# Second layer of the block in seven products: four of seven units summed over two neighbouring quads in a PSUM bank

## The chip, the cores and the metric

One core of a Trainium2 chip. The metric is device microseconds of one execution. Engines: PE is TensorE (PEld its weight loads), DVE VectorE, ACT ScalarE, POOL GpSimd, and SP issues nearly all DMAs.

## The reference, cut

```python
x = performer_attention(q, k, v, omega)          # [2304, 512]
P = sinkhorn(exp(x @ w_gate))                    # [2304, 8], 8 rounds
out = zeros(2304, 512)
for e in range(8):                               # w1: 8 x 512 x 1024, w2: 8 x 1024 x 512
    h = maximum(x @ w1[e], 0)
    out += P[:, e:e+1] * (h @ w2[e])
h = out @ w_in                                   # w_in 512 x 2048, float64 in DRAM
return (h - tanh(h)) @ w_out                     # w_out 2048 x 512, float64 in DRAM
```

All in float32 accuracy: each factor is held as a high part (float32r) and a low part, and a product is three matmuls, high by high, high by low, low by high.

## The kernel before, in words

Attention runs first (to about 170 us). Then come stages: the sum over the eight experts for three blocks of 768 tokens, s = 0, 1, 2, and the last two layers for the same three blocks.

**The expert stages.** The 8 x 1024 hidden columns are cut into 32 quads of 256 columns. For a quad the first layer (512 x 256 weights against 512 x 768 tokens, seen as 2 x 2 blocks) is made with seven block products in place of eight, in Winograd's form. Each product is six matmuls of 128 x 128 by 384 columns (`product`, L1089); three PSUM banks a, b and e take them. In s = 0 the second layer is plain (L1356). In s = 1 and s = 2 it too is made with seven products: `quad7` makes seven forms of h, H[0] to H[6], each high and low half (`high` on ACT, `low` on POOL, L1173), and each unit i multiplies H[i] with a summed piece of w2 and adds to the accumulator `xacc[i]` (SBUF, two halves d of 128 x 384). At the end of a block `join` adds the seven accumulators to the four blocks of the result and stores them.

**Order around the change.** The program order of each engine is the order in which the code is run (manual schedule). A quad has seven steps: a first-layer product, then `between(k)`, which runs unit UORD[k] of the previous quad (`Second.run(k)`), UORD = 5, 0, 4, 3, 2, 1, 6, and then two ticks. A unit is two groups of three matmuls, one for each half d, each in a bank of its own. For d = 1 ACT copies the accumulator into the bank beforehand (`load`, L1248), the matmuls add to it, and ACT copies it back (L1269). For d = 0 DVE adds the bank to the accumulator (L1275); in s = 2 three of the seven are "light": ACT copies the bank out (L1279) and POOL adds it (L1280). After a unit `post(k)` makes the next forms of h: the subtractions that give t1 (L1216) and t3 (L1220) on DVE, one on POOL (L1222), t4 (L1227), and their splits. PSUM's eight banks are five for the first layer (tag q) and three for the second (tag l). h has nine buffers.

**Weights.** A generator, `weights()`, is advanced once by each tick. For quad a it loads the first layer's seven pieces u (split once in s = 0 and kept in DRAM, `st1`) and the second layer's seven pieces y of quad a - 1 (`st2`). Two y pieces share a tile; there are six tiles, and a tile is granted when both units of the tile six before are used. During s = 1 four of the seven y pieces (units 1, 2, 3, 5) are new: POOL makes four sums of raw w2 (`sums_of`, L202 to L205), ACT and POOL (for unit 2 DVE) split each (L89, L92), and the piece is stored for s = 2 when two later ones wait. `convert` turns w_in and w_out from float64 bits to float32 on DVE (L1054 to L1066), ACT and POOL in the later part of s = 0 and in s = 2, one step on 24 of 32 and 18 of 32 ticks. The last stage's loads of them wait until all is converted.

## Time and profile before

| | us |
|---|---|
| median of 3 runs | 2267.24 (2261.35 to 2270.09) |
| the profiled execution | 2264.46 |
| its span, first to last instruction | 2262.4 |
| PE busy in the span | 2071.4 |
| DVE, ACT, POOL busy | 1731.7, 1376.3, 1607.7 |

PE's busy time counts every stretch in which a matmul is under way; matmuls overlap, so it is no measure of how fast they follow each other. The times of steps are read from the starts of matmuls in the timeline.

### The profile page before, as it was taken

What the parts mean: (1) busy time and instruction counts of PE and PEld (TensorE: products, weight loads), DVE (VectorE), ACT (ScalarE), POOL (GpSimd) and SP (SyncE); (2) the same over time, 40 slices, a digit from 0 to 9 for tenths busy, and PEclk for the clock granted to TensorE, in tenths of its full rate; (3) what the DMA queues carried; (4) which work ended last, traced back from release to release, by engine and by line L of the source; (5) the groups of instructions that cost most, each with busy time, mean ns of one, the idle gap of its engine ahead of it and who ended that gap; (6) DMA issues with size and microseconds to landing.
All of it is one profiled execution on the core that took longest, in us unless ns stands there. A gap on an engine that the chain in (4) does not pass through costs nothing.

```text
span 2262.4 us, 37383 instructions
## 1 busy us (share of the span) xinstructions
PE 2071.4 (92%) x11408; PEld 1902.6 (84%) x11408; DVE 1731.7 (77%) x3277; ACT 1376.3 (61%) x3337; POOL 1607.7 (71%) x1961
## 2 busy tenths in 40 slices
PE   9999999999997988888888688888888879999999
PEld 7777988999987888888888688888888868998998
DVE  8884868888864666666666587888778769999997
ACT  7883333444433666666666366666666667888885
POOL 7866878878744777777767677777777797565552
PEclk9999999999998999999999799999999999999999
DMA  6538787788756778777787577877778723132210
GB/s 167 145 116 281 272 281 265 265 285 284 260 188 212 239 245 289 239 256 252 243 261 234 183 249 251 276 253 245 238 249 251 226 98 110 53 116 75 90 52 33
DMA packets 341368, 470.85 MB, mean 208 GB/s; under 512 B 70944, under 2 KB 164784, under 8 KB 341168
## 3 DMA queue, kind: packets, MB, share of 16 engines
q1 hardware_dynamic: 335568, 461.85, 62.4%
q10 hardware_dynamic: 5600, 6.61, 0.8%
q8 instruction: 91, 1.49, 0.3%
q14 instruction: 109, 0.89, 0.1%
HBM read 328.29 MB, written 140.06 MB: 207 GB/s over the span
## 4 chain that ended last, share of the span: by engine, by line
PE 49%; DVE 15%; POOL 13%; ACT 7%; DMA 7%; issue 6%; SPq 2%; DVEq 0%; POOLq 0%; ACTq 0%
PE l L1356 16%; PE b L1089 8%; PE Y L1261 6%; PE e L1089 5%; PE X L1261 5%; PE p L1318 4%; PE a L1089 3%; DMA st<-y 3%; POOL h L1173 3%; ACT h L1170 2%; POOL tmp L513 1%; POOL h L1222 1%; SPq L252 1%; POOL s L203 1%; DVE t L1339 1%
## 5 line engine op out<-in xcount | busy, mean ns | idle before, releaser
L1356 PE MATMUL l<-v,h 128*128 128x512 f32 x2016 | 485.1, 394 | 8.0 <-ACT h L1344 2.7
L1356 PEld LDWEIGHTS l<-v,h 128*128 128x128 f32 x2016 | 377.0, 189 | 86.6 <-ACT h L1344 4.3
L1261 PE MATMUL Y<-h,y 128*128 128x384 f32 x1290 | 313.9, 347 | 113.6 <-ACT Y L1248 66.9
L1269 ACT COPY seven<-Y 128x384 f32<-128x384 f32 x430 | 206.8, 481 | 301.0 <-PE Y L1261 297.3
L1089 PE MATMUL b<-x,u 128*128 128x384 f32 x1728 | 357.5, 342 | 10.1 <-DVE t L1183 9.7
L1261 PE MATMUL X<-h,y 128*128 128x384 f32 x1398 | 327.9, 345 | 35.7 <-DVE seven L1275 24.1
L1261 PEld LDWEIGHTS Y<-h,y 128*128 128x128 f32 x1290 | 226.9, 190 | 145.5 <-ACT Y L1248 87.4
L1089 PEld LDWEIGHTS b<-x,u 128*128 128x128 f32 x1728 | 314.3, 193 | 15.7 <-DVE t L1183 10.0
L1173 POOL TENSOR_TENSOR h<-t,h 128x384 fp32r<-128x384 f32 x224 | 232.4, 1038 | 104.0 <-ACT h L1170 55.9
L1275 DVE TENSOR_TENSOR seven<-X,seven 128x384 f32<-128x384 f32 x345 | 190.2, 552 | 151.2 <-PE X L1261 149.4
L1261 PEld LDWEIGHTS X<-h,y 128*128 128x128 f32 x1398 | 254.8, 193 | 45.9 <-DVE seven L1275 31.4
L1173 POOL TENSOR_TENSOR h<-h,h 128x384 fp32r<-128x384 f32 x192 | 204.0, 1063 | 47.9 <-ACT h L1170 46.6
L1089 PE MATMUL a<-x,u 128*128 128x384 f32 x1152 | 233.5, 337 | 1.5 <-ACT u L89 1.5
L1089 PE MATMUL e<-x,u 128*128 128x384 f32 x1152 | 232.7, 336 | 0.0
L1318 PE MATMUL p<-x,u 128*128 128x384 f32 x1152 | 211.7, 339 | 0.0
L1248 ACT COPY Y<-seven 128x384 f32<-128x384 f32 x430 | 209.3, 487 | 0.4
L1318 PEld LDWEIGHTS p<-x,u 128*128 128x128 f32 x1152 | 205.2, 190 | 3.4
L1089 PEld LDWEIGHTS a<-x,u 128*128 128x128 f32 x1152 | 204.0, 189 | 2.8 <-ACT u L89 2.2
L1089 PEld LDWEIGHTS e<-x,u 128*128 128x128 f32 x1152 | 204.4, 189 | 0.0
L92 POOL TENSOR_TENSOR v<-rs,v 128x256 fp32r<-128x256 f32 x176 | 144.3, 848 | 64.4 <-ACT v L89 57.8
L1345 POOL TENSOR_TENSOR h<-t,h 128x384 fp32r<-128x384 f32 x94 | 97.5, 1037 | 121.7 <-ACT h L1344 116.5
L1170 ACT CAST h<-t 128x384 fp32r<-128x384 f32 x224 | 115.5, 516 | 50.2 <-POOL t L1227 24.3
(245 smaller groups left out, 4060.5 us busy)
## 6 DMA issues: line engine op xcount, KB each, us to landing
u<-st SPq DMA_DIRECT2D x448, 256.0 KB, 4.5
y<-st SPq DMA_DIRECT2D x320, 256.0 KB, 4.1
st<-u SPq DMA_DIRECT2D x224, 256.0 KB, 4.3
rs<-in_moe_w_dram SPq DMA_DIRECT2D x128, 256.0 KB, 3.6
st<-y SPq DMA_DIRECT2D x128, 256.0 KB, 4.8
st<-v SPq DMA_DIRECT2D x96, 256.0 KB, 5.3
rq<-in_moe_w_dram SPq DMA_DIRECT2D x32, 512.0 KB, 4.9
rqi<-win SPq DMA_DIRECT2D x24, 512.0 KB, 4.6
```

The source lines that it names most:

```text
L92: eng.tensor_tensor(dst[:, 1, i : i + w], src[:, i : i + w], dst[:, 0, i : i + w].bitcast(F32), ALU.subtract)
L203: G.tensor_tensor(s2, s1, a11, ALU.subtract)
L1089: nc.tensor.matmul(ps[:, :TB], u[:, wi, c], x[:, xi, c], start=(start and m == 0), stop=(stop and m == 5), skip_group_check=True,)
L1170: nc.scalar.copy(H[k][:, 0], src)
L1173: eng.tensor_tensor(H[k][:, 1], src, H[k][:, 0].bitcast(F32), ALU.subtract)
L1248: nc.scalar.copy(ps, xacc[UORD[k]][:, 1])
L1261: nc.tensor.matmul(ps, u[:, wi, d * P : (d + 1) * P], h[:, hi], start=(j == 0 and not pre), stop=(j == 2), skip_group_check=True,)
L1269: nc.scalar.copy(X[:, d], ps)
L1275: nc.vector.tensor_tensor(X[:, d], ps, X[:, d], ALU.add)
L1318: nc.tensor.matmul(ps, u1[f + i][:, wi, c], ux[state["x0"] + 2 * t + i][:, xi, c], start=(m == 0), stop=(m == 11))
L1345: nc.gpsimd.tensor_tensor(lo, s, hi.bitcast(F32), ALU.subtract)
L1356: nc.tensor.matmul(ps, hh[f][:, hi, t : t + P], u2[n + f][:, wi], start=(f == 0 and i == 0), stop=(f == len(hh) - 1 and i == 2),)
```

## The change

The second layer is planned by slots (7 for a quad) in place of `Second`. Units 0 and 6 of an even quad and of the odd one before it, and units 5 and 4 of an odd quad and of the even one before it, are summed in one bank: a group of six matmuls for each half d, in two different slots. Both halves of these are preloaded and copied back by ACT. Units 1, 2 and 3 stay two groups of three a quad; their d = 0 is added by DVE, their d = 1 goes through ACT for unit 2 (s = 1) or all three (s = 2), and through DVE otherwise. Light adds are gone. A quad's units run in slots 1 to 8 after its end (1, 2: the first pair unit; 3, 4, 5, 6; 7 is the next quad's slot 0) in place of 0 to 6. The third subtraction (t3) moves into `post(0)`. The joins come one or two slots later. In s = 1 and s = 2 there are four and four banks; before and after, five and three. h has five buffers for halves that are used up in the next quad and four for those held for two. Unit 5's new piece of an even quad is split into a spare place and only stored, and is read back for the next, odd quad; the other pieces are asked for in the order in which they are used. Stores are issued three ticks after the piece. Conversion in s = 0 stops one quad later; in s = 2 its steps are finer (8 a piece in place of 6) and taken on 22 of 32 ticks. The nine slots after the last quad run within the first four pieces of the last stage.

```diff
+    stores = []
+    def store(dst, src):
+        stores.append([2, dst, src.bitcast(F32)])
+    def send(age):
+        for x in stores:
+            x[0] -= 1
+        while stores and stores[0][0] < age:
+            nc.sync.dma_start(*stores.pop(0)[1:])
+    def second_units(R):
+        r = R % NQ
+        if r == 0:
+            return [(0, R), (3, R), (2, R), (1, R), (6, R)]
+        if r % 2 == 0:
+            return [(0, R - 1), (0, R), (3, R), (2, R), (1, R), (6, R - 1), (6, R)]
+        units = [(5, R - 1), (5, R), (4, R - 1), (4, R), (3, R), (2, R), (1, R)]
+        return units[:4] + [(0, R)] + units[4:] + [(6, R)] if r == NQ - 1 else units
...
                 if a == 1:
-                    flush()
+                    send(9)
...
-                for i in range(7):
-                    if a < NG:
+                R = a - 1
+                units = second_units(R) if a else []
+                if fresh and R % 2 == 0:
+                    units.append((5, -1))
+                for i in range(max(7, len(units))):
+                    if a < NG and i < 7:
...
-                    if not a:
...
-                    m = 7 * (a - 1) + i
+                    o, g = units[i]
...
+                    u = two[:, m % 2]
+                    if g < 0:
+                        spentw.add(m)
                     else:
-                        two = uw[m - 1][1]
-                    u, o = two[:, m % 2], UORD[i]
-                    uw[m] = u, two
-                    st = st2[(a - 1) % NQ][:, o]
-                    if fresh and o in src:
+                        uw[o, g] = u, m
+                    m += 1
+                    if fresh and (g < 0 or g == R and o in (1, 2, 3, 5)):
                         split(u, src[o], nc.vector if o == 2 else G)
-                        store(st, u)
+                        store(st2[R][:, o], u)
                         yield None
                     else:
-                        nc.sync.dma_start(u.bitcast(F32), st)
+                        nc.sync.dma_start(u.bitcast(F32), st2[g % NQ][:, o])
...
+    def set_banks(name, nq, nl):
+        banks.close()
+        ppm[:] = [banks.enter_context(tc.tile_pool(name=name, bufs=nq, space=PSUM, reuse_waits="tile")), nl]
+    set_banks("ppm", 5, 3)
...
+    hp_ = ctx.enter_context(tc.tile_pool(name="hp", bufs=5))
...
             V.tensor_scalar(cf, hi.bitcast(F32), big, -big, ALU.min, ALU.max)
+            if fine:
+                yield
             V.tensor_scalar(t, c, 3, 0x3FFFFFFF, ALU.logical_shift_left, ALU.bitwise_and)
             yield
             V.scalar_tensor_tensor(h, c, 0xC0000000, t, ALU.bitwise_and, ALU.bitwise_or)
+            if fine:
+                yield
...
+    def htile(name, held=None, shape=[P, 2, TB], dt=F32R):
+        if held is None:
+            held = hcount[0] % 9 % 2
+            hcount[0] += 1
+        return hp_.tile(shape, dt, tag="k" if held else "h", name=name, bufs=4 if held else 5)
...
+            H[k] = htile(f"h7_{g}_{k}", k in ((0, 6) if g % 2 else (5, 4)))
...
             if k == 0:
+                t1[0], t3[0] = tmp(3, f"t1_{g}"), keep("t3")
+                V.tensor_tensor(t1[0], B, h11, ALU.subtract)
+                V.tensor_tensor(t3[0], h22, B, ALU.subtract)
                 low(4, h21, own)
-                t1[0] = tmp(3, f"t1_{g}")
-                V.tensor_tensor(t1[0], B, h11, ALU.subtract)
             elif k == 1:
                 hsplit(3, t1[0])
-                t3[0] = keep("t3")
-                V.tensor_tensor(t3[0], h22, B, ALU.subtract)
...
-    class Second:
...
+    Hs, plan = {}, {}
+    def at(t):
+        return plan.setdefault(t, ([], [], []))
+    def slot(t):
+        for f in at(t + 1)[0]:
+            f()
+        for f in [f() for f in at(t)[1]]:
+            f()
+        for f in at(t)[2]:
+            f()
+        plan.pop(t)
+    def group(t, i, gs, d, act, first, last):
+        cell = []
+        def pre():
+            cell.append(lbank(f"Y{t}_{i}_{d}")[:, :TB])
+            nc.scalar.copy(cell[0], xacc[i][:, d])
+        def run():
+            ps = cell[0] if cell else lbank(f"X{t}_{i}_{d}")[:, :TB]
+            n = 0
+            for g in gs:
+                need((i, g), uw, "w")
+                for wi, hi in ((0, 0), (0, 1), (1, 0)):
                     nc.tensor.matmul(
-                        ps, u[:, wi, d * P : (d + 1) * P], h[:, hi], start=(j == 0 and not pre), stop=(j == 2),
-                        skip_group_check=True,
+                        ps, uw[i, g][0][:, wi, d * P : (d + 1) * P], Hs[g][i][:, hi],
+                        start=(n == 0 and not cell), stop=(n == 3 * len(gs) - 1), skip_group_check=True,
                     )
-                todo.append((d, ps, pre))
-            spentw.add(m)
-            for d, ps, pre in todo:
-                if pre or self.first and d:
-                    nc.scalar.copy(X[:, d], ps)
-                elif self.first:
-                    nc.vector.tensor_copy(X[:, d], ps)
-                elif not d and k in light:
-                    last = ps
+                    n += 1
+                if last:
+                    spentw.add(uw[i, g][1])
+            def evict():
+                if act:
+                    nc.scalar.copy(xacc[i][:, d], ps)
+                elif first:
+                    nc.vector.tensor_copy(xacc[i][:, d], ps)
                 else:
-                    nc.vector.tensor_tensor(X[:, d], ps, X[:, d], ALU.add)
-            self.post(k)
-            if last is not None:
-                t = tmp(2, f"x{self.g}_{k}")
-                nc.scalar.copy(t, last)
-                nc.gpsimd.tensor_tensor(X[:, 0], t, X[:, 0], ALU.add)
...
+            return evict
+        if act and not first:
+            at(t)[0].append(pre)
+        at(t)[1].append(run)
...
+        at(t + 4)[2].append(add(5, 3, G))
+        at(t + 5)[2].append(add(3, 2, G))
+        at(t + 6)[2].extend((add(4, 0, G), put(4, 0, 0)))
+        at(t + 7)[2].extend(
+            (add(1, 0, V), add(5, 1, V), put(5, 0, 1), add(3, 1, G), put(3, 1, 1), add(2, 1, G))
+        )
+        at(t + 8)[2].extend((add(6, 2, G), put(6, 1, 0), lambda: xdone.add((1, s))))
...
+    def second_layer(s, R, post):
+        r, t = R % NQ, 7 * (R + 1)
+        for k in range(5):
+            at(t + k)[2].append(lambda k=k: post(k))
+        upper = (1, 2, 3) if s == 2 else (2,)
+        def one(k, i):
+            first = r == 0
+            group(t + k, i, [R], 1, i in upper, first, False)
+            group(t + k, i, [R], 0, False, first, True)
+        def two(k, k2, i):
+            group(t + k, i, [R - 1, R], 1, True, r == 1, False)
+            group(t + k2, i, [R - 1, R], 0, True, r == 1, True)
+        if r == 0:
+            one(1, 0)
+        elif r % 2 == 0:
+            two(1, 2, 0)
+            two(6, 7, 6)
+        else:
+            two(1, 2, 5)
+            two(3, 6, 4)
+        if r % 2:
+            one(4, 3)
+            one(5, 2)
+            one(7, 1)
+        else:
+            one(3, 3)
+            one(4, 2)
+            one(5, 1)
+        if r == 0:
+            one(6, 6)
+        elif r == NQ - 1:
+            one(3, 0)
+            one(8, 6)
+            join(s, t)
...
+        send(0)
...
+        set_banks("ppl", 5, 3)
...
-                if Q == NQ - 5:
+                if Q == NQ - 4:
...
+                if s == 1 and Q == 0:
+                    set_banks("ppn", 4, 4)
...
-                    pace[4] = 18
+                    pace[4] = 22
...
+                    slot(7 * g + k)
+                    if not g:
...
+                Hs[g], post = quad7(g, Q == NQ - 1, pbs[0][0], s == 1, between)
+                second_layer(s, g, post)
...
+                ready.extend(lambda t=t: slot(t) for t in range(7 * NG, 7 * NG + 9))
```

## Rows read from the trace of the kernel before

**Rows 1.** The page, part 1: busy us, share of the span and instructions of each engine.

```profile
PE 2071.4 (92%) x11408; PEld 1902.6 (84%) x11408; DVE 1731.7 (77%) x3277; ACT 1376.3 (61%) x3337; POOL 1607.7 (71%) x1961
```

**Rows 2.** Windows by stage: stretch, its length, busy us (count) of PE, PEld, DVE, ACT, POOL, clock, DMA.

```profile
733.01:1234.93 501.92, 444.15 (x2438) 425.32 (x2437) 322.70 (x614) 312.94 (x755) 361.47 (x406) 0.99 0.76 252
1234.93:1306.97 72.04, 52.37 (x254) 49.53 (x253) 42.77 (x71) 32.88 (x73) 45.89 (x37) 0.83 0.59 191
1306.97:1807.87 500.90, 442.72 (x2438) 426.73 (x2438) 395.57 (x660) 324.67 (x763) 390.39 (x384) 0.99 0.78 250
1807.87:1866.00 58.13, 41.25 (x200) 37.86 (x200) 38.59 (x52) 37.90 (x88) 52.02 (x48) 0.91 0.29 98
```

**Rows 3.** Timeline, PE, a step without a wait: start, length, line, operation, count.

```profile
1012.75 1.20 PE L1089 MATMUL b<-x,u 128*128 128x384 f32 x6
...
1014.84 1.20 PE L1089 MATMUL e<-x,u 128*128 128x384 f32 x6
```

**Rows 4.** Waits of PE, s = 1, then s = 2: us in total, times, longest.

```profile
PE Y L1261 <- POOL h L1173: 41.2, 29, 2.8
PE Y L1261 <- ACT Y L1248: 16.6, 29, 0.9
...
PE Y L1261 <- ACT Y L1248: 36.8, 29, 2.9
PE X L1261 <- DVE seven L1275: 21.1, 19, 1.5
```

**Rows 5.** Groups by line, ACT, s = 1: shapes, count | busy us, mean ns | idle before.

```profile
L1248 ACT COPY Y<-seven 128x384 f32<-128x384 f32 x203 | 98.9, 487 | 0.4
```

**Rows 6.** Groups by line, DVE, s = 2.

```profile
L1275 DVE TENSOR_TENSOR seven<-X,seven 128x384 f32<-128x384 f32 x116 | 63.9, 551 | 28.2 <-PE X L1261 28.1
L1055 DVE TENSOR_SCALAR cw_False<-cw_False 128x256 uint32<-128x256 uint32 x36 | 30.0, 833 | 1.2
```

**Rows 7.** Groups by line, POOL, s = 2.

```profile
L1173 POOL TENSOR_TENSOR h<-t,h 128x384 fp32r<-128x384 f32 x116 | 120.7, 1040 | 27.7 <-ACT h L1170 23.9 <-DMA y<-st 2.7
...
L1280 POOL TENSOR_TENSOR seven<-x,seven 128x384 f32<-128x384 f32 x86 | 91.2, 1060 | 47.0 <-ACT x L1279 44.4 <-DMA y<-st 2.1
```

**Rows 8.** Timeline, POOL and PE, s = 1, steps 3 and 4 of one quad.

```profile
998.80 0.74 POOL L92 TENSOR_TENSOR y<-s,y 128x256 fp32r<-128x256 f32 x1
...
999.62 0.74 POOL L202 TENSOR_TENSOR s<-rs 128x256 f32<-128x256 f32 x1
...
1002.97 0.98 POOL L1222 TENSOR_TENSOR h<-h,t 128x384 f32<-128x384 f32 x1
...
1004.97 0.62 PE L1261 MATMUL Y<-h,y 128*128 128x384 f32 x2 [2.25 <-POOL h L1173]
```

**Rows 9.** Timeline, ACT and PE, s = 2, step 0 of one quad.

```profile
1793.26 0.51 ACT L1170 CAST h<-t 128x384 fp32r<-128x384 f32 x1
1793.67 0.48 ACT L1248 COPY Y<-seven 128x384 f32<-128x384 f32 x1
...
1794.21 0.81 PE L1261 MATMUL Y<-h,y 128*128 128x384 f32 x3 [0.73 <-ACT Y L1248]
```

**Rows 10.** A window of 10 us, and DMA issues of the page (part 6, us to landing).

```profile
866.00:876.00 10.00, 9.76 (x56) 9.44 (x55) 6.78 (x14) 7.51 (x19) 5.57 (x7) 1.00 1.06 405
...
y<-st SPq DMA_DIRECT2D x320, 256.0 KB, 4.1
...
st<-y SPq DMA_DIRECT2D x128, 256.0 KB, 4.8
```

**Rows 11.** Timeline, DVE, POOL and PE, second quad of s = 2.

```profile
1295.36 0.29 DVE L1054 TENSOR_SCALAR cw_False<-r 128x256 f32<-128x256 f32 x1 [12.78 <-DMA r<-in_moe_w_in_dram]
...
1296.51 1.97 PE L1089 MATMUL b<-x,u 128*128 128x384 f32 x5 [9.70 <-DVE t L1183]
...
1297.45 1.13 POOL L1222 TENSOR_TENSOR h<-h,t 128x384 f32<-128x384 f32 x1 [11.18 <-DVE t L1220]
```

**Rows 12.** Timeline, SP, first load of the converted w_in.

```profile
1800.10 0.43 SPq L142 DMA_DIRECT2D rqi<-win  x1
```

More of the change, by code (lines that the diff above doesn't have):

```diff
@@ L161, in weights @@
                     jobs.append(("s", -1, lambda f=f: load_slab(wout32[f * P : (f + 1) * P, :])))
-        ahead, stores = [], []
-        def store(dst, src):
-            stores.append((dst, src.bitcast(F32)))
-            flush(2)
-        def flush(n=0):
-            while len(stores) > n:
-                nc.sync.dma_start(*stores.pop(0))
+        ahead = []
         n_last = 3 * NGM * GF // 2 * NSB
@@ L253, in weights @@
                         n1 += 1
-                    if not a:
+                    if i >= len(units):
                         continue
-                    m = 7 * (a - 1) + i
+                    o, g = units[i]
                     if m % 2 == 0:
@@ L1032, in performer_moe_kernel, with convert @@
     halt, cxp = [False], []
-    def convert(raws, work):
+    def convert(raws, work, fine):
         V = nc.vector
@@ L1150, in quad @@
         tick()
-        return [h[k] for k in ((0, 0), (1, 0), (0, 1), (1, 1))]
+        return [[h[k]] for k in ((0, 0), (1, 0), (0, 1), (1, 1))]
     def quad7(g, last, pb, fresh, between):
@@ L1233, in performer_moe_kernel @@
     xacc = {}
-    class Second:
-        def __init__(self, s, g, H, post, first, final):
-            self.s, self.g, self.H, self.post, self.first, self.final = s, g, H, post, first, final
-            self.loaded = {}
-        def on_act(self, k, mode):
-            return k in mode and not self.first
-        def load(self, k, mode):
-            if k < 7 and self.on_act(k, mode):
-                ps = self.loaded[k] = lbank(f"Y{self.g}_{k}")[:, :TB]
-                nc.scalar.copy(ps, xacc[UORD[k]][:, 1])
-        def run(self, k, light=()):
-            i, m = UORD[k], 7 * self.g + k
-            need(m, uw, "w")
-            u, h, X = uw[m][0], self.H[i], xacc[i]
-            todo, last = [], None
-            for d in (1, 0):
-                ps = self.loaded.pop(k, None) if d else None
-                pre = ps is not None
-                if not pre:
-                    ps = lbank(f"X{self.g}_{k}_{d}")[:, :TB]
-                for j, (wi, hi) in enumerate(((0, 0), (0, 1), (1, 0))):
+    Hs, plan = {}, {}
@@ new lines, in run, with join, add, put @@
+            return evict
+        if act and not first:
+            at(t)[0].append(pre)
+        at(t)[1].append(run)
+    def join(s, t):
+        V, G = nc.vector, nc.gpsimd
+        to = xd[1].rearrange("(i c p) t -> p i c t", p=P, i=2)
+        def add(x, y, eng):
+            return lambda: eng.tensor_tensor(xacc[x], xacc[x], xacc[y], ALU.add)
+        def put(x, r, c):
+            o = s * SBT + c * TB
+            return lambda: nc.sync.dma_start(to[:, r, :, o : o + TB], xacc[x])
+        at(t + 4)[2].append(add(5, 3, G))
[5 more added lines that the diff above has]
+        at(t + 8)[2].extend((add(6, 2, G), put(6, 1, 0), lambda: xdone.add((1, s))))
@@ L1321, in shrink @@
                     m += 1
-        h = htile(f"h{name}")
-        hi, lo = h[:, 0], h[:, 1]
+        h = []
         u, ga, gb = (tmp(i, f"t{i}_{name}") for i in range(3))
         if early:
-            th, s = (hp_.tile([P, TB], F32, tag="h", name=f"{i}{name}") for i in ("th", "s"))
+            th, s = (htile(f"{i}{name}", None, [P, TB], F32) for i in ("th", "s"))
         else:
@@ L1343, in third @@
         def third():
+            h.append(htile(f"h{name}"))
+            hi, lo = h[0][:, 0], h[0][:, 1]
             nc.scalar.copy(hi, s)
@@ L1539, in performer_moe_kernel @@
                     load_p(*((s, e + 1) if e < E - 1 else (s + 1, 0)))
-                mode, light = range(7), (0, 3, 6) if s == 2 else ()
                 def between(k):
-                    if prior:
-                        prior.load(k + 1, mode)
-                        prior.run(k, light)
-                    else:
+                    slot(7 * g + k)
+                    if not g:
                         second(2)
@@ L1550, in between @@
                     tick()
-                if prior:
-                    prior.load(0, mode)
-                H, post = quad7(g, Q == NQ - 1, pbs[0][0], s == 1, between)
-                prior = Second(s, g, H, post, Q == 0, Q == NQ - 1)
+                Hs[g], post = quad7(g, Q == NQ - 1, pbs[0][0], s == 1, between)
+                second_layer(s, g, post)
                 if Q == NQ // 4:
@@ L1562, in performer_moe_kernel @@
                     tick()
-                odd = (1, 3, 5)
-                def tail(k):
-                    prior.run(k)
-                    prior.load(k + 1, odd)
-                ready.extend(lambda k=k: tail(k) for k in range(7))
+                ready.extend(lambda t=t: slot(t) for t in range(7 * NG, 7 * NG + 9))
                 ready.append(last_turn)
@@ L1588, in performer_moe_kernel @@
                         else:
-                            second(2)
+                            second((3, 2, 3, 2)[f])
                     for t in range(3):
```

46 lines of the change are left out of this document (14 added, 32 removed).

## The prediction

> **What bounds the kernel now.** I read the busy shares first. TensorE is busy for 92% of the span [rows 1], which seems to leave 8%, some 190 us, in all. The windows by stage show where they lie [rows 2]: in the sweeps over the second and the third token block, which run both layers in seven products (s = 1 and s = 2), TensorE idles about 58 us each, and the changes of stage after each idle 20 and 17 us. The step view is sharper than the busy time. A step (one of seven in a quad) is six first-layer and six second-layer matmuls, and where nothing is waited for a new step starts every 2.09 us, 1012.75 to 1014.84 [rows 3]; seven make 14.6 us. Each of the two windows holds 29 quads (203 preloads at seven a quad [rows 5], 116 adds at four a quad [rows 6]): 501.9/29 = 17.31 us a quad in s = 1 and 500.9/29 = 17.27 us in s = 2. So 29 x 2.7 = 79 us and 78 us are lost to waits in these two windows. That is the most that the change can win there.
>
> The Trainium skill says the same of the first figure (Perfetto Trace Analysis, Identifying the Most-Contended Engine): matmul busy time is a bad measure of headroom, because matmuls are pipelined. The rows agree: 58 us idle by busy time against 79 us by steps in one window.
>
> The waits then say on whom TensorE waits [rows 4]. In s = 1: 41.2 us on a low half of h from POOL and 16.6 us on ScalarE's preload of a bank. In s = 2: 36.8 us on the preload and 21.1 us on VectorE's add that frees a bank. In s = 1 the POOL wait is one event in each second quad: the four weight sums, 999.62 to 1002.97, stand in POOL's queue ahead of the subtraction and the split of h for unit 2, and TensorE idles 2.25 us [rows 8]. In s = 2 the preload wait is step 0 of every quad: ScalarE has to make the high half of unit 4 (1793.26) before the preload (1793.67), and the matmuls start at 1794.21 after 0.73 us [rows 9].
>
> **Part 1, evictions.** The matmul count stays (42 in the second layer a quad), so TensorE's work is unchanged. Per pair of quads 28 half-banks were emptied; now 4 units x 2 halves = 8 groups of six matmuls and 3 units x 2 quads x 2 halves = 12 of three, 20 in all. In s = 1 ScalarE makes 20 preloads and copies back a pair where it made 28, so 4 fewer a quad, 4 x 0.49 = 1.9 us [rows 5]; VectorE makes 5 adds a quad where it made 7, 2 x 0.55 = 1.1 us [rows 6]. In s = 2 ScalarE falls from 17 copies a quad (three of them the light ones) to 14, 1.4 us; VectorE from 4 adds to 3, 0.55 us; POOL loses its three adds, 3 x 1.06 = 3.2 us [rows 7]. From rows 2 the loads a quad become, s = 1: ScalarE 10.8 to 8.9, VectorE 11.1 to 10.0, POOL 12.5 unchanged; s = 2: ScalarE 11.2 to 9.8, VectorE 13.6 to 13.0, POOL 13.5 to 10.3. All lie under 14.6 us, so none of this is a gain by itself; it is slack.
>
> **Part 2, one step later.** Step 0 of a quad now runs a unit (1, or half of 6) of the quad before the last, whose h has long been split, and its preload, if any, is issued in step 6, ahead of the high half of unit 4. The first unit that needs the new quad is at step 1. In rows 9 the preload was late by 0.73 to 1 us; at step 1 it has 2.09 us more. This removes the step 0 waits except where VectorE itself ran late; I leave 0.3 us a quad in s = 2.
>
> **Part 3, four and four banks.** A fourth bank for the second layer, and only one group in pair steps, means that an eviction may be about two steps late before TensorE feels it. The 21.1 us on VectorE's add should go. The price is on the other side: with four first-layer banks the third product of a quad takes the bank that the previous quad's second product held, so it waits for the two subtractions that now both stand in step 0. After an odd second-layer quad VectorE first makes the add for unit 1; its matmuls end 2.1 us after the step began, then add, subtraction, subtraction, about 0.55 us each by rows 6 (all three in 1.7 us as they overlap a little), 3.9 us, against 4.18 us at which step 2 begins. Covered by 0.3 us. If VectorE is late by a conversion instruction (0.83 us, rows 6), 0.5 us is lost; I put 0.2 us a quad in s = 2 and nothing in s = 1, where no conversion runs.
>
> The h buffers stay nine, five and four. A buffer that is held for the second quad is written again after its last use; only unit 4's high half comes close, since it waits for step 6's matmuls (1.04 us behind the product), while VectorE needs 1.1 us for its source anyway. Nothing; if not covered, some 0.1 us a quad.
>
> **Part 4, the weight pieces.** Following the yields of the weight generator, two ticks a step, a tile being granted when both units of the one six before are used: before, the four sums come after step 1 of one quad and step 2 of the next. Now, in s = 1, they come after step 4 in one quad, where nothing needs POOL for three steps, and after step 6 in the other, because the tile for unit 6 and the extra split of unit 5 waits for unit 4, which is spent only at step 6. There POOL's order is split of 5, four sums, low half of unit 0, and unit 0 of that quad is needed in the next step 1. From the start T of that step 6: the copy back ends at T+2.7, the piece's high half at T+3.2, its low half (0.74, rows 8) at T+3.9, the sums (3.35 from 999.62 to 1002.97) at T+7.2, the low half of unit 0 (1.04, rows 7) at T+8.2. TensorE wants it at T + 2x2.09 + 1.04 + 0.52 + 0.17 = T+5.9. It waits 2.35 us, once a pair: 1.2 us a quad. Between nothing (sums hidden) and 2.6 us a quad (as many waits as now) I take 1.2, from the row.
>
> The seven units and the extra split make 16.5 transfers of 256 KB a quad in s = 1 instead of 16. At the rate shown in one 10 us stretch, 405 GB/s [rows 10], they need 10.7 us of 15.8. The look-ahead shrinks: before, a piece was asked for 10 to 12 steps ahead, now 6 to 9 (12.5 to 19 us), against 4.1 us of landing time [rows 10]. Covered. A store that is issued three ticks later holds nobody up unless SP reaches it before POOL has written; then the loads behind it on SP wait some 2 us, inside the same cover. The conversion's finer steps cost no instruction more: 22/32 of 14 ticks over 8 steps is 1.20 pieces a quad (36/29 = 1.24 before).
>
> **Part 5, edges.** From s = 1 to s = 2, 72 us hold three quads (28 us more than their steps) and 9.7 us of waiting on VectorE, which itself sat 12.8 us on the first conversion load, behind the joined sums' stores on SP's queue [rows 11]. The joins now come one or two steps later and units 5 and 4 of the first new quad are only evicted a quad later; but that load is still behind the stores. Between +5 and -12 us I take -6. At the end of s = 2 there is a loss. 37 pieces are left (one more quad of conversion in s = 0 makes 27 instead of 26 there), each eight steps: 298 steps, of 31 x 14 x 22/32 = 298. The conversion ends with the last quad, not a quad and a half earlier, so the first load of w_in, now at 1800.10 [rows 12], comes some 10 us later relative to the stage. Its landing and first split would be felt by about 6 us, partly paid back since these splits no longer crowd the last quad: +4, between 0 and +10.
>
> **Sum.** s = 1: 14.6 + 1.2 + 0.1 (stray loads) = 15.9 us, 29 x (17.31 - 15.9) = -41 us. s = 2: 14.6 + 0.3 + 0.2 + 0.05 = 15.15 us, 29 x (17.27 - 15.15) = -61 us. Edges -6 and +4. Total -104 us. The profiled execution took 2264.5 us (span 2262.4), the median of the three runs is 2267.2, 2.8 us above, within their spread of 9. 2264.5 - 104 = **2160 us**.
>
> **Rivals.**
> A, fuller cover: if the sums find POOL idle early enough or the wait at step 1 is short, s = 1 comes to 15.0 us and s = 2 to 14.85: 67 + 70 + 10 us, **2117 us**. For it: POOL has 3.5 us to spare a quad.
> B, VectorE becomes the bound in s = 2. One conversion instruction takes 0.29 us where POOL idles [rows 11] and 0.83 us in the stretch [rows 6]. Six of them at 1.2 pieces make 7.2 a quad; if each grows to a whole POOL instruction on top of its own (1.04 [rows 7] + 0.29 = 1.33 us), VectorE needs 13.0 + 7.2 x 0.5 = 16.6 us a quad, and s = 2 wins only 29 x 0.67 = 19 us: 2264.5 - 41 - 19 - 2 = **2202 us**. Against it: POOL has 3.2 us less to do there.
> The Trainium skill states the mechanism (SBUF — State Buffer, Who interferes with whom): VectorE and GpSimd share a port pair that one of them holds for a whole instruction while the other is blocked. By it the same conversions packed into shorter quads would meet POOL more often; the two durations, 0.29 and 0.83 us, agree with it.
> C, nothing moves: the low halves from POOL stay the limit at their old 2.6 us a quad and edges eat the rest, about **2262 us**. Against it: the s = 2 waits have no POOL in them [rows 4].
> D, slower: weights come too late. Unit 5 is stored and read back one quad on; the load cannot start before the store has landed, and SP's later loads queue behind it. Store and load are 4.8 + 4.1 = 8.9 us [rows 10], the cover is seven steps, 14.6 us. From there each microsecond more costs one in each of the 16 pairs of s = 1. It outweighs the 104 us from a round trip of 14.6 + 104/16 = 21 us; at 23 us the time is about **2295 us**.
>
> **How the numbers follow.** Forecast 0.55 (2125 to 2195), A 0.17, B 0.18, C 0.04, D 0.06. Range for 8 in 10: 2112 to 2215, which takes in A's and B's times and the bounds of parts 4 and 5. A measurement of this kernel tells about 0.5%, 11 us, from no change. Faster 0.55 + 0.17 + 0.18 = 0.90, same 0.04, slower 0.06.
>
> **What would show it.** Right: step 0 at 2.09 us in nearly all quads; no wait of TensorE on VectorE's add in s = 2; in s = 1 one wait on POOL per pair of quads, at step 1, of some 2.4 us, with the four sums just ahead of it in POOL's queue; 20 half-banks emptied a pair. Wrong: waits of a first-layer product on VectorE's subtraction (four banks too few), waits on a DMA of a y or u piece (D), VectorE over 90% busy in s = 2 (B), or a stall of more than 10 us ahead of the first matmul of the last stage.

## The result and the profile after

The changed kernel takes **2169.85 us** (median of 4 runs, 2166.42 to 2173.33), the kernel before 2268.13 us in the same comparison: a ratio of 0.957, with a 95% interval of 0.9546 to 0.9598. That is 98 us faster. The profiled execution has a span of 2171.5 us against 2262.4, 90.9 us less. The forecast was 2160 us, 104 us below the profiled execution of the kernel before, in a range from 2112 to 2215. Beside e9 and e10 of the experiments, two of the seven runs of the kernel before took 7239 and 3356 us at granted clocks of 0.27 and 0.56, and the ratios given for e9 and e10 leave these two out.

The answer to rows 1 (the page's first part: busy us, share of the span, instructions) shows that TensorE does the same work. ScalarE, VectorE and GpSimd issue 227, 87 and 93 instructions less.

```profile
PE 2050.5 (94%) x11408; PEld 1908.8 (88%) x11408; DVE 1633.4 (75%) x3190; ACT 1273.0 (59%) x3110; POOL 1498.8 (69%) x1868
```

The answer to rows 2, the windows by stage of the changed kernel (stretch, length, busy us and count of PE, PEld, DVE, ACT and POOL, granted clock, DMA share, GB/s), cut at the same products:

```profile
732.83:1203.93 471.10, 441.15 (x2432) 432.87 (x2431) 294.52 (x555) 258.52 (x632) 350.63 (x401) 0.97 0.82 274
1203.93:1282.52 78.59, 54.22 (x260) 51.95 (x260) 44.77 (x73) 27.52 (x61) 47.38 (x41) 0.78 0.59 200
1282.52:1712.71 430.19, 424.96 (x2432) 423.34 (x2431) 318.68 (x619) 280.72 (x667) 293.93 (x296) 0.99 0.82 286
```

The stage s = 1 gave 30.8 us (501.9 to 471.1), s = 2 gave 70.7 us (500.9 to 430.2), and the three quads between them took 6.6 us more (72.0 to 78.6). The last quad and the stage behind it lie outside these rows. Cut at the same products, the last quad takes 14.7 us (18.7 before) and all behind it 444.2 us (435.8), together 4.3 us more. With 0.2 us ahead of the first window the sum is -30.8 + 6.6 - 70.7 + 4.3 - 0.2 = -90.8 us.

In 29 quads s = 2 now takes 14.83 us a quad, of which seven steps at 2.08 us are 14.56: it runs at TensorE's own pace. The waits of TensorE (us in total, times, longest), in s = 1 and then in s = 2, answer rows 4:

```profile
PE Y L1294 <- POOL h L1206: 28.7, 14, 2.7
PE X L1294 <- DVE seven L1308: 0.4, 2, 0.2
...
PE Y L1294 <- ACT Y L1286: 5.0, 1, 5.0
```

The preload wait of every quad is gone, and so is VectorE's add. What is left in s = 2 is one event, at the end of quad 73 of the 96: ScalarE stood behind a cast whose tile of the next stage's x had not landed (timeline of ScalarE; the bracket is the idle time ahead and what ended it).

```profile
1401.54 0.83 ACT L88 CAST x<-xt 128x768 fp32r<-128x768 f32 x1 [5.71 <-DMA xt<-xd]
```

In s = 1 one wait is left in each second quad, 14 of them, and the timeline shows the order that rows 8 showed in another place: the four sums, then the low half. GpSimd first, then TensorE:

```profile
748.23 0.74 POOL L213 TENSOR_TENSOR s<-rs 128x256 f32<-128x256 f32 x1
...
750.55 0.73 POOL L216 TENSOR_TENSOR s<-rs 128x256 f32<-128x256 f32 x1
751.24 1.00 POOL L1206 TENSOR_TENSOR h<-h,h 128x384 fp32r<-128x384 f32 x1
...
752.29 0.63 PE L1294 MATMUL Y<-h,y 128*128 128x384 f32 x2 [1.96 <-POOL h L1206]
752.75 2.09 PE L1122 MATMUL e<-x,u 128*128 128x384 f32 x6
754.64 1.92 PE L1294 MATMUL Y<-h,y 128*128 128x384 f32 x6
```

The last two lines show something that the forecast did not have: after the wait, six matmuls take 2.09 us in place of 1.20. The windows of the step with the wait, of the step behind it, and of the same step of a later quad behind a wait of the same length (2.01 us) have the granted clock as their third figure from the end:

```profile
748.43:752.75 4.32, 2.36 (x14) 2.04 (x13) 2.61 (x6) 0.88 (x3) 3.65 (x5) 1.00 0.12 37
752.75:756.40 3.65, 3.65 (x14) 3.65 (x14) 0.00 (x0) 1.20 (x3) 2.42 (x3) 0.53 0.71 243
785.72:787.82 2.10, 2.10 (x13) 2.10 (x13) 0.00 (x0) 1.20 (x3) 0.87 (x1) 1.00 0.93 337
```

At 0.53 the engine ran nearly all of the second of these steps at the lower of its two levels (1.2 GHz in place of 2.4). Step 2 of the 14 quads took 2.97 to 3.65 us in eight of them and 2.08 to 2.10 us in six.

At the edge from s = 1 to s = 2 VectorE still stands on the conversion's first load, and TensorE behind VectorE, as in rows 11 but longer. SP, VectorE and TensorE in that order:

```profile
1257.92 0.99 SPq L1325 DMA_DIRECT2D xd<-seven  x2
1259.21 0.93 SPq L1068 DMA_DIRECT2D r<-in_moe_w_in_dram  x2
...
1267.94 0.29 DVE L1078 TENSOR_SCALAR cw_False<-r 128x256 f32<-128x256 f32 x1 [15.98 <-DMA r<-in_moe_w_in_dram]
...
1268.76 2.29 PE L1122 MATMUL b<-x,u 128*128 128x384 f32 x6 [16.27 <-DVE t L1216]
```

### The profile page after: what moved, and what is told of

The parts are those of the page before. It is cut to its first block, busy times and chain, and to the rows that moved or that the text cites. A ratio compares the mean times of both kernels' runs of the same rounds, so it can differ in the third digit from the quotient of the medians.

```text
span 2171.5 us, 37317 instructions
## 1 busy us (share of the span) xinstructions
PE 2050.5 (94%) x11408; PEld 1908.8 (88%) x11408; DVE 1633.4 (75%) x3190; ACT 1273.0 (59%) x3110; POOL 1498.8 (69%) x1868
## 4 chain that ended last, share of the span: by engine, by line
PE 67%; DVE 9%; POOL 8%; DMA 8%; issue 4%; ACT 3%; SPq 1%; POOLq 0%; ACTq 0%; DVEq 0%
PE l L1429 18%; PE Y L1294 12%; PE b L1122 11%; PE e L1122 8%; PE a L1122 7%; PE p L1390 7%; PE X L1294 5%; DMA u<-st 2%; DMA st<-y 2%; POOL tmp L529 1%; POOL h L1206 1%; POOL eq L689 1%; DMA xd<-xo 1%; DVE seven L1308 1%; DVE t L1410 1%
## 5 line engine op out<-in xcount | busy, mean ns | idle before, releaser
L1294 PE MATMUL Y<-h,y 128*128 128x384 f32 x1812 | 391.4, 344 | 47.8 <-POOL h L1206 32.2
L1294 PEld LDWEIGHTS Y<-h,y 128*128 128x128 f32 x1812 | 328.3, 194 | 58.4 <-POOL h L1206 39.0
L1304 ACT COPY seven<-Y 128x384 f32<-128x384 f32 x364 | 175.2, 481 | 311.0 <-PE Y L1294 309.5
L1122 PE MATMUL e<-x,u 128*128 128x384 f32 x1152 | 238.3, 342 | 1.9 <-DVE t L1249 1.9
L1294 PE MATMUL X<-h,y 128*128 128x384 f32 x876 | 191.1, 340 | 8.8 <-ACT h L1203 5.1
L1286 ACT COPY Y<-seven 128x384 f32<-128x384 f32 x364 | 176.3, 488 | 0.3
L1294 PEld LDWEIGHTS X<-h,y 128*128 128x128 f32 x876 | 157.1, 191 | 12.9 <-ACT h L1203 5.4
L1308 DVE TENSOR_TENSOR seven<-X,seven 128x384 f32<-128x384 f32 x256 | 135.7, 548 | 36.8 <-PE X L1294 36.7
```

Source lines behind the costliest of these rows:

```text
L1122: nc.tensor.matmul(ps[:, :TB], u[:, wi, c], x[:, xi, c], start=(start and m == 0), stop=(stop and m == 5), skip_group_check=True,)
L1286: nc.scalar.copy(cell[0], xacc[i][:, d])
L1294: nc.tensor.matmul(ps, uw[i, g][0][:, wi, d * P : (d + 1) * P], Hs[g][i][:, hi], start=(n == 0 and not cell), stop=(n == 3 * len(gs) - 1), ...
L1304: nc.scalar.copy(xacc[i][:, d], ps)
L1308: nc.vector.tensor_tensor(xacc[i][:, d], ps, xacc[i][:, d], ALU.add)
```

## The experiments

Ten kernels ran, all timed in three rounds against the kernel before. The table cuts every trace at the same products: the 29 quads of s = 1, the three quads of the edge, the 29 quads of s = 2, the last quad, and the rest (us, from the profiled executions; medians of the timed runs in the last two columns).

| kernel | s = 1 | edge | s = 2 | last quad | rest | median us | ratio to before |
|---|---|---|---|---|---|---|---|
| before | 501.9 | 72.0 | 500.9 | 18.7 | 435.8 | 2268.1 | 1 |
| after | 471.1 | 78.6 | 430.2 | 14.7 | 444.2 | 2169.9 | 0.957 |
| e1, sums one step later | 423.6 | 70.6 | 429.4 | 14.6 | 444.3 | 2118.2 | 0.935 |
| e2, later step and banks, no pair sums | 422.5 | 64.3 | 437.9 | 14.6 | 449.9 | 2125.0 | 0.938 |
| e3, pair sums, not later | 575.9 | 79.5 | 501.2 | 17.9 | 443.9 | 2352.2 | 1.038 |
| e4, five and three banks | 485.7 | 75.9 | 432.0 | 17.2 | 446.2 | 2189.8 | 0.966 |
| e5, stores at once | 469.5 | 78.6 | 430.0 | 14.6 | 445.7 | 2169.1 | 0.958 |
| e6, conversion's load early | 470.6 | 68.8 | 428.7 | 15.8 | 438.4 | 2159.8 | 0.954 |
| e7, pace 24 | 469.6 | 75.8 | 431.6 | 14.7 | 437.5 | 2164.3 | 0.956 |
| e8, e1 with e6, pace 26 | 424.3 | 65.4 | 439.8 | 14.7 | 435.1 | 2113.3 | 0.934 |
| e9, later step alone, five and three | 425.2 | 66.0 | 472.6 | 18.0 | 446.1 | 2161.3 | 0.954 |
| e10, e1 with e6, pace 24 | 423.4 | 64.5 | 433.1 | 14.7 | 438.3 | 2109.4 | 0.932 |

**The sums' place (e1).** The theory is that of the forecast's part 4: the four sums stand ahead of a low half that TensorE needs. One yield more puts them behind it.

```diff
                 if fresh:
                     if a < NQ:
+                        if R % 2 == 0:
+                            yield None
                         src = sums_of(raws)
                         yield None
```

> The changed kernel, with one more yield ahead of the four weight sums of every second quad of s = 1, so that in program order they come behind the low half of unit 0 instead of ahead of it. Theory (the place of the sums in POOL's queue is the whole remaining wait of s = 1): the 16 waits of about 2.3 us at step 1 go, and with them the stretches of halved TensorE clock that follow some of them (about 1.2 us in 9 of them). The 29-quad window of s = 1 falls from 471 to 425-432 us, the time from 2170 to about 2127 us. Rival (POOL has too much work in s = 1, 12.5 us a quad, and any place of the sums delays some unit): the wait moves to the units of steps 3 and 4, and the time stays at 2150 us or more.

It took 2118.2 us, some 52 us less than the changed kernel and 9 less than expected, and the window of s = 1 is:

```profile
733.73:1157.28 423.55, 422.97 (x2431) 420.63 (x2431) 296.07 (x555) 259.48 (x632) 353.84 (x401) 1.00 0.88 306
```

TensorE's waits in it fall from 29.1 us to 0.6. GpSimd's work is the same, 353.84 us against 350.63: only its order changed. TensorE's busy time, with as many matmuls, falls from 441.15 to 422.97 us, and its clock rises from 0.97 to 1.00. So of the 47.5 us that s = 1 lost to the sums' place, 28.5 were waiting and 18 were longer busy time. Of these 18 some 14 are the lower clock: a mean of 0.97 over 471.10 us, where e1 has 1.00 (by the trace's clock records 27 us at the lower level, and none in e1's window). The other 4 stand in the 14 steps that wait, which count about 2.36 us busy where a step without a wait counts 2.08, at a clock of 1.00. Eight us more came back at the edge, whose first quad held one more such wait, of 3.4 us.

**The later step without the pair sums (e2).** It separates the parts 2 and 3 from part 1. The units, the evictions and the light adds are those of the kernel before, run one slot later. What e2 shares with the changed kernel besides is the third subtraction in `post(0)`, the stores and the finer conversion steps.

```diff
     def second_units(R):
...
+        return [(o, R) for o in UORD]
...
+        first = r == 0
+        for k, i in enumerate(UORD):
+            group(t + k + 1, i, [R], 1, True, first, False)
+            group(t + k + 1, i, [R], 0, False, first, True, s == 2 and k in (0, 3, 6) and not first)
```

> The later step without the pair sums: every unit is two groups of three matmuls again, d = 1 through ScalarE, d = 0 through VectorE, light adds in s = 2 as in the kernel before (28 half-banks emptied a pair), in the old order of units, but each one step later, with four and four banks and the new stores and conversion steps. Theory (the step and the bank are what removed the waits; the evictions were never the limit): s = 2 at about 15.2 us a quad, s = 1 at about 15.0 because unit 2 has 2.09 us more cover against its 2.5 us wait; time 2135-2155 us, no slower than the changed kernel. Rival (fewer evictions carry the gain): s = 2 stays above 16 us a quad, time 2190 us or more.

2125.0 us, 10 under the range expected: without any pair sum it is 45 us faster than the changed kernel. In s = 1 it takes 422.5 us, as e1 does (423.6), since it has no wait on the sums. In s = 2 it is 7.7 us slower than the changed kernel; the waits there are small, 16 in 29 quads:

```profile
PE Y L1287 <- ACT Y L1279: 7.5, 15, 1.0
PE X L1287 <- DVE seven L1308: 1.2, 1, 1.2
```

So with the later step and the banks in place the pair sums are worth 7.7 us in s = 2, and in s = 1, by where they put the weight sums, they cost 48.6 us.

**The pair sums without the later step (e3).** The plan starts a slot earlier, and what it would have asked for in a slot already gone is issued at once.

```diff
         upper = (1, 2, 3) if s == 2 else (2,)
+        t -= 1
...
+        t += 1
+        for f in at(t)[0]:
+            f()
+        at(t)[0].clear()
```

> The pair sums without the later step: the changed kernel with every unit one step earlier (steps 0 to 7), the preload of step 0 issued after the high half of unit 4, as before. Theory: the preload wait of step 0 is back in s = 2, 0.7 to 1 us a quad (about 30 us in all), and in s = 1 the first unit meets POOL's sums 2.09 us earlier, 4.4 us a pair in place of 2.3 (about 33 us); time 2225-2240 us. Rival (the pair sums carry the gain): within 15 us of the changed kernel's 2170 us.

2352.2 us, 3.8% slower than the kernel before. The direction was right; the size was missed by 110 us and more. The waits in s = 1 and then in s = 2:

```profile
PE Y L1294 <- POOL h L1206: 61.6, 42, 2.6
PE Y L1294 <- ACT Y L1286: 20.9, 15, 1.6
PE X L1294 <- POOL h L1206: 13.9, 28, 0.6
...
PE Y L1294 <- POOL h L1206: 23.6, 43, 0.7
PE Y L1294 <- ACT Y L1286: 23.3, 28, 1.8
```

The expectation counted the step 0 waits of the kernel before and left out that every unit of a quad is now due a step earlier. Units 3, 2 and 1 of an even quad are due even a step earlier than in the kernel before (steps 2 to 4 of the odd quad that follows, in place of 3 to 5), and their three low halves miss their step in each odd quad of s = 2, as here in steps 2 and 3 of one of them:

```profile
1691.22 0.61 PE L1294 MATMUL Y<-h,y 128*128 128x384 f32 x2 [0.64 <-POOL h L1206]
...
1694.21 0.62 PE L1294 MATMUL Y<-h,y 128*128 128x384 f32 x2 [0.62 <-POOL h L1206]
```

So e3 shows that the changed kernel, with its four banks and its pair sums, loses all its gain when its units come a step earlier. It is not the kernel before with the pair sums added, since the changed kernel runs units 3, 2 and 1 of even quads in steps 3 to 5, as before, and only the others later. That its s = 2 takes as long as that of the kernel before (501.2 and 500.9 us) is chance: in the kernel before, TensorE has no wait on GpSimd in s = 2 [rows 4].

**The banks (e4, e9).** e4 is the changed kernel with `set_banks("ppn", 5, 3)` in place of 4, 4; e9 is e2 with the same edit.

> The changed kernel with five first-layer and three second-layer banks in s = 1 and s = 2, as before. Theory (the fourth bank removed TensorE's waits on VectorE's add): waits of the single groups in steps 3 to 5 on the adds return in part, some 0.2-0.7 us a quad, time 2176-2190 us. Rival (one group in the pair steps already made enough room): no change, 2170 us within 5; if the four first-layer banks cost something, a little faster.

> The second layer one step later without any sum over two quads (2125.0 with four and four banks), now with five banks for the first products and three for the second layer, as the kernel before has them. So it differs from the kernel before by the later step and the order of the stores alone. If the later step by itself takes away the waits for late banks, because VectorE's adds have a step more in which to give a bank back, the time is 2125 to 2135. If the fourth bank is what took away the 21.1 us that s=2 of the kernel before waited for VectorE's adds, these come back: 2140 to 2155. If the later step does nothing without the fourth bank, the time is above 2200.

e4 took 2189.8 us, 20 more than with four and four; in the profiled executions 14.6 of it in s = 1, where the waits on VectorE's add came back as its theory had it (8.9 us, 0.4 with four banks), and only 1.8 in s = 2. e9 took 2161.3 us, 36 more than e2, in none of the three ranges that were written for it (2125 to 2135, 2140 to 2155, over 2200) and nearest to the second. Its waits in s = 2 are those on VectorE's add, more of them than in rows 4 (e4 in s = 1, then e9 in s = 2):

```profile
PE X L1294 <- DVE seven L1308: 8.9, 8, 1.8
...
PE X L1287 <- DVE seven L1308: 30.0, 32, 1.8
PE X L1287 <- ACT seven L1304: 0.6, 1, 0.6
```

With these two the stage s = 2 can be read as a small grid:

| s = 2, us | five and three banks | four and four banks |
|---|---|---|
| no later step, no pair sums | 500.9 (before) | |
| later step, no pair sums | 472.6 (e9) | 437.9 (e2) |
| later step, pair sums | 432.0 (e4) | 430.2 (after) |

The later step without the two gives 28.3 us; the moved third subtraction and the finer conversion steps, which e9 has too, are in this figure, and no run takes them apart. The fourth bank then gives 34.7, or the pair sums 40.6; the second of the two adds only 7.7 or 1.8. They are two cures for one wait: a bank more, or fewer half-banks to empty. In s = 1, where no conversion runs, the same step gives 76.7 us (501.9 to 425.2, e9); the four sums move with it there, since the weight tiles come free a step later, and that was not varied by itself.

**The stores (e5).** `store`, which puts away the split weight pieces, issues its DMA at once.

```diff
-        stores.append([2, dst, src.bitcast(F32)])
+        nc.sync.dma_start(dst, src.bitcast(F32))
```

> The changed kernel with its store of xT issued in the step of its piece again, not three steps later; everything else stays. If the delay of the stores gave nothing, as the prediction had it (the weight pieces are issued far enough ahead), the time stays at 2170, within 4 us. If it was part of the gain, because loads stood behind waiting stores on SP's queue, the time rises over 2180, and TensorE or the joins on GpSimd show waits for weight pieces in the second layer's stages. A third way: the stores that are put off stand in front of the conversion's loads at the edge, so that issuing them at once gives some us back in quads 63 to 65.

2169.1 us, within 1 us of the changed kernel: the delay of the stores, three ticks, neither gave nor cost anything.

**The edge and the end of the conversion (e6, e7).** e6 issues the conversion's first load at the start of the second quad of s = 2, ahead of the stores of the joined sums that are due in it (on SP at 1252.89 ahead of 1254.22, where the changed kernel has 1259.21 behind 1257.92), and begins the conversion's other steps after that quad; e7 lets the conversion end earlier.

```diff
-                    pace[4] = 22
+                    pace[4] = 23
...
+                    next(bg[0])
                 pace[3] = Q < 2 or Q == NQ - 1
-                pace[2] = False
+                pace[2] = s == 2 and Q == 1
```

> The changed kernel with the conversion's first load issued one quad earlier (at the start of the second quad of s=2), and the conversion's steps begun after that quad; its pace is adapted from 22 to 23. Quads 63 to 65 took 78.6 us after the change, against 72.0 before; VectorE stood 15.98 us on that load at the edge, and TensorE 16.27 us behind VectorE. If the order of this one load is what the edge costs, quads 63 to 65 fall by 12 to 16 us and the time comes to 2152 to 2160. If the first quad of the stage is held by the joins on GpSimd in any case, the wait moves to them, and the time stays at 2166 or above.

```diff
-                    pace[4] = 22
+                    pace[4] = 24
```

> The changed kernel with the pace of the conversion at 24 instead of 22, so that it ends about two quads earlier; nothing else is changed. The stretch after quad 95 took 444.2 us after the change against 435.8 before, and its first product waited 5.86 us for ScalarE. If the second layer's quicker quads leave the conversion too little time and its rest runs into the stage behind it, that stretch falls by about 6 us and the time comes to 2164, between 2161 and 2167. If the wait there has nothing to do with how far the conversion is, the time stays at 2170, within 2 us; and if the denser conversion slows the quads of s=2 by as much, s=2 rises by some 5 us and nothing is won.

e6 took 2159.8 us. The edge fell by 9.8 us, less than the 12 to 16 expected, because two other waits came up behind the one removed. The first is the one that the expectation named as its rival: GpSimd makes a low half only behind the joins, and TensorE waits 4.63 us for it. The second is ScalarE's: it copies the new stage's first sums into the tiles of the old ones, waits until these are stored, and TensorE waits for ScalarE's next cast (GpSimd and TensorE, then ScalarE and TensorE):

```profile
1251.52 2.13 POOL L1321 TENSOR_TENSOR seven<-seven,seven 128x768 f32<-128x768 f32 x1
1253.62 0.99 POOL L1206 TENSOR_TENSOR h<-t,h 128x384 fp32r<-128x384 f32 x1
...
1254.66 1.97 PE L1294 MATMUL X<-h,y 128*128 128x384 f32 x5 [4.63 <-POOL h L1206]
...
1264.24 0.48 ACT L1304 COPY seven<-X 128x384 f32<-128x384 f32 x1 [15.61 <-DMA xd<-seven]
...
1265.18 0.45 PE L1294 MATMUL X<-h,y 128*128 128x384 f32 x1 [4.07 <-ACT h L1203]
```

e7 took 2164.3 us, as expected. The rest fell by 6.7 us. The first load of the converted w_in now comes ahead of the last product (1708.51, where the last quad begins at 1708.47), not behind it (1730.39, where the last quad begins at 1712.71); the wait of TensorE at the first matmul of the last stage, 5.86 us, is gone. SP of the changed kernel and its TensorE, then SP of e7 and its TensorE:

```profile
1730.39 1.07 SPq L141 DMA_DIRECT2D rqi<-win  x2
...
1734.90 4.58 PE L1390 MATMUL p<-x,u 128*128 128x384 f32 x12 [5.86 <-ACT u L88]
```

```profile
1708.51 0.43 SPq L141 DMA_DIRECT2D rqi<-win  x1
...
1724.59 2.24 PE L1390 MATMUL p<-x,u 128*128 128x384 f32 x12
```

**All together (e8, e10).** Both have e1's edit and e6's; the pace is 26 in e8 and 24 in e10.

> The changed kernel with three edits: the four sums of every second quad of s=1 one step later (2118.2 by itself), the conversion's first load one quad earlier, and the conversion's pace at 26 instead of 22. The gains lie in different stretches, so if they add up the time is 2118 less 12 to 16 us at the edge less about 6 us behind quad 95, that is 2092 to 2104, at about 2098. If the edge's gain is lost because the quads before it now come faster (quads 63 to 65 were already down to 70.6 us with the sums later), only half of the edge's gain is left and the time is 2106 to 2112.

> The changed kernel with the sums of s=1 one step later, the conversion's first load one quad earlier and the conversion's pace at 24, not 26 as in the run with all three (2113.3). There s=2 took 439.8 us against 429.4 with the sums later alone, with waits of TensorE for ScalarE's preloads in quads 67 to 86. If it is the dense conversion that delays ScalarE, s=2 comes back to 429 to 432 us and the time to 2104, between 2101 and 2108. If it is the early start of the conversion, or the sums' new place, the time stays within 3 us of 2113.

e8 took 2113.3 us, not 2092 to 2104: the edge fell from e1's 70.6 to 65.4 us, about half of what e6 gained there, and s = 2 rose to 439.8 us. Its waits of TensorE there:

```profile
PE Y L1296 <- ACT Y L1288: 12.4, 7, 5.6
```

e10, with a pace of 24, took 2109.4 us, the fastest of all (0.932 of the kernel before, interval 0.930 to 0.934), 1.4 us over the range expected. s = 2 came down to 433.1 us, with 6.5 us of those waits left. In these two profiled executions, then, the denser conversion carries most of what e8 lost in s = 2 (6.7 of 10.4 us). Whether the 4 us between e10 and e1 in s = 2 come from the pace or from the conversion's earlier start was not told apart.

## Why the prediction was right, and where its terms were off

The sum was -104 us and the profiled executions differ by 90.9. The two terms of the stages miss by some 10 us each, in opposite directions; that they cancel is luck, and what is left of the difference is the edge. By the terms:

- **s = 2, forecast 15.15 us a quad, measured 14.83** (9 us better). Step 0 takes 2.08 us in all but the first of these quads and the one behind the event in quad 73, no add of VectorE is waited for, and 20 half-banks are emptied a pair: 199 preloads and 201 copies back in 29 quads are 13.8 a quad (14 forecast), 86 adds are 2.97 (3 forecast). The allowances of 0.3 us for a late VectorE and 0.2 us for the third product's bank were not used: 430.19 us are 8.0 above 29 times 14.56, and the single event, a wait of 4.95 us and slower steps behind it, lengthens quads 73 and 74 to 20.72 and 16.08 us, 7.7 together.
- **s = 1, forecast 15.9, measured 16.24** (10 us worse). Part 4's place of the sums and the step at which TensorE would feel them were right, and e1 shows it by undoing it. The wait was put at 2.35 us a pair and measured 28.7/14 = 2.05. What the term lacked is the longer busy time that goes with the wait, 18 us by e1, 1.3 us a pair, most of it the lower clock: the term mis-sized is that one, 3.3 us a pair in place of 2.35. The reading under it was a little off: of the 29 waits on GpSimd in rows 4, 14 are of 2.2 to 2.8 us in each second quad and 15, of 0.5 to 1.2 us, lie in the quads between.
- **The edge, forecast -6 between +5 and -12, measured +6.6.** This step failed, beyond its worse end. Part 5 said itself that the load is still behind the stores, and then counted a gain from the later joins. With the joins a step or two later the opposite came: the load is issued 14.15 us behind the first product of its quad (1259.21, 1245.06) where it was 11.84 (1285.29, 1273.45), and VectorE's wait went from 12.78 [rows 11] to 15.98 us. Of the 78.6 us, 8.0 are the sums' place again (e1: 70.6), and some 10 are the load's (e6: 68.8); both edits together gave 13.2 (e8: 65.4).
- **The end of s = 2, forecast +4 between 0 and +10, measured -4.0 for the last quad and +8.3 behind it, +4.3.** The stall of "about 6 us" ahead of the last stage is the 5.86 us above, and e7 removes it by ending the conversion earlier. (37 pieces of eight steps are 296 steps, not 298; nothing hangs on it.)
- **Stores harmless, weights in time.** e5 shows the first; the weight pieces cause no wait of TensorE in either stage's rows. So rival D does not stand.

Of the rivals, A (2117 us) is near what e1 makes: s = 1 at 14.61 and s = 2 at 14.81 us a quad, the fuller cover, 2118.2 us. It was one yield away. That the totals agree to 1 us is luck: A had s = 1 at 15.0, some 11 us more, and 10 us of gain at the edges, where e1 has none. B, VectorE as the bound of s = 2, did not come: VectorE was busy for 318.68 of 430.19 us. B read its price from two instructions: the 0.29 us at the edge are L1054's, the 0.83 us are L1055's; L1054 itself took 0.72 us in the stretch. On the changed kernel's line L1081 the instruction of 0.83 us took 0.39 us, and in e2 (line L1074) 0.50 us (groups by line, VectorE, s = 2: the kernel before, the changed kernel, e2):

```profile
L1054 DVE TENSOR_SCALAR cw_False<-r 128x256 f32<-128x256 f32 x36 | 25.7, 715 | 0.4
...
L1081 DVE TENSOR_SCALAR cw_False<-cw_False 128x256 uint32<-128x256 uint32 x35 | 13.8, 393 | 0.5
...
L1074 DVE TENSOR_SCALAR cw_False<-cw_False 128x256 uint32<-128x256 uint32 x35 | 17.4, 496 | 0.3
```

e2 has the finer conversion steps and, with the light adds, GpSimd's old load (389.65 us in s = 2, 390.39 before [rows 2], 293.93 in the changed kernel). The six instructions of a piece take 4.68 us before, 4.28 in e2 and 3.38 in the changed kernel. So 0.4 us of the fall come without any change in GpSimd's work, and 0.9 us with it. The Trainium skill (SBUF — State Buffer, Who interferes with whom) has B's rule, that VectorE and GpSimd hold each other up at a shared port pair; the 0.9 us agree with it. No run here changed GpSimd's load alone (e2 differs in its evictions too), so that this is the cause is argued, not shown. C (nothing moves) fell with s = 2.

Part 1 said that the fewer evictions are slack and no gain by themselves. That holds for the four banks that the change brings along (7.7 us in s = 2); with three it would have been wrong, since there they are worth 40.6. Part 2 was undersold: it was argued from the preload in s = 2, but in s = 1, without any pair sum and with the old banks, the later step and what moves with it (e9) took 76.7 us out, the waits on GpSimd's low halves included. In s = 1 the later step with four banks reached 422.5 us without pair sums (e2), so that all that the pair sums did there was to put the weight sums in the wrong place.

What stays open: why the clock fell behind eight of 14 waits of nearly the same length and not behind the other six; how much of the gain in s = 2 belongs to the finer conversion steps; and what e3's 74 us in s = 1 above the kernel before come from one by one. By its window, 42 of them are idle time of TensorE and 32 longer busy time (476.06 us in place of 444.15 [rows 2]), at a granted clock of 0.96.

## What to carry to other kernels

A consumer that is moved one step later in an in-order schedule pays for itself where several engines each miss its start by about a step or less (here by 0.2 to 2.9 us, at a step of 2.09); a bank more and fewer evictions were then two cures for the same wait, and the second added little. After such a change, read where the side work (here four sums on GpSimd) now stands in its queue, ahead of which split, since a single yield was worth 52 us here. At a change of stage follow the chain load, store, copy-back to its end: with one wait removed, the next one took over a part of the gain.

## What was not expected of the hardware

A wait of some 2 us cost more than itself. In s = 1 of the changed kernel 14 waits of 28.7 us in total went with 18 us more busy time of TensorE for as many matmuls (441.15 against 422.97 us in e1), some 14 of it by the lower clock, with the granted clock at 0.53 in a step behind such a wait, and at 1.00 in the same step behind another one (2.01 us). At the edge the wait of 16.27 us was followed by blocks of six matmuls of 2.29, 2.12 and 2.12 us in place of 1.20 (timeline of TensorE):

```profile
1274.41 2.12 PE L1122 MATMUL a<-x,u 128*128 128x384 f32 x6
1276.33 2.12 PE L1294 MATMUL X<-h,y 128*128 128x384 f32 x6
1278.25 1.30 PE L1122 MATMUL b<-x,u 128*128 128x384 f32 x6
```
